# The second unit's columns move from the plain mixing stage to the seven-product stage

## Chip, cores and metric

The kernel runs on one core of a Trainium2 chip. The metric is the device time of one execution in microseconds (us); lower is better. A core has a matrix engine (PE, with its weight loads shown apart as PEld), three elementwise engines (DVE, ACT, POOL), and DMA queues that SP and ACT issue.

## What is computed

The input is `x` of 8 batches x 3008 tokens x 256 channels. The reference is a spectral block, then a token and channel mixer:

```
X = np.fft.rfft(x, axis=1)
Yr = Xr @ w_r - Xi @ w_i + b_r
Yi = Xr @ w_i + Xi @ w_r + b_i
...
x = np.fft.irfft(soft_threshold(Y), n=3008, axis=1)
h = np.maximum(x.transpose(0, 2, 1) @ w_tok1, 0.0) @ w_tok2
u = x + h.transpose(0, 2, 1)
out = u + np.maximum(u @ w_ch1, 0.0) @ w_ch2
```

`w_ch1` is 256 x 1536 and `w_ch2` 1536 x 256. Every product is made of three matmuls (`mm3`): high part by high part, high by low, low by high.

## The kernel before

The eight batches form five **units**: unit 0 is batch 0, unit 1 is batch 1, and units 2, 3 and 4 are two batches each. Each unit passes through two kinds of work.

The **spectral** work (generator `spectral(u)`) turns a unit's tokens into `b_d[u]` (the inverse transform's first half, in DRAM) and into `g_d[u]` (the rectified token product, in DRAM). For unit 1 it begins with thirteen steps of a transform of 47 points (`dft47`, line 299). Then come twelve steps for unit 1 and twenty-four for a later unit: `forward` (tile `px`, line 492), `mix` (tiles `pm`, lines 206 to 208), `inverse` (tile `pi`) and `tokens` (tile `gp`). Beside the steps of units 1 to 3 the next unit's 47-point transform is made (`beside`, tile `p`). Each step loads from DRAM and stores to it: `a_d`, `in_x`, `w_d` and `in_e` for unit 1, `ws_d` and `es_d` for the later units.

The **mixing** work takes a unit's columns (tokens) in chunks. Groups of 4 or 5 slots of 94 tokens (`groups`, cut by `sizes`) are made by `half_u`: token product and inverse transform in one PSUM bank (`pu`, or `sz` in the later stage), copied to `uf`. Then a chunk goes through `w_ch1` and `w_ch2`, in one of two ways:
- **plain** (`channel`): chunks of at most 512 columns. Per chunk, 12 blocks of `first` (tile `ph`) and `second` (tile `po`), with 72 + 72 matmuls as wide as the chunk. ACT makes `hh` and DVE `hlo` of each block.
- **seven-product** (`channel7`): chunks of at most 1024 columns, each cut in halves of columns, channels and hidden rows, with seven products of quarters for eight (a Strassen-Winograd scheme). Per chunk, 6 pairs x 2 layers x 7 products x 3 = 252 matmuls of half the chunk's width. The sums run on DVE, ACT and POOL. Its weight sums are made once, by `weigh` and `weigh2`, beside the last plain chunk (tiles `a`, `sf`, `ws`, lines 1028 to 1049); there the spectral pools are closed too (`open_seven`), and the new chunk's first operands are made (`first_u`, `rest_u`: tiles `t` and `ub`).

Engines run their instructions in the order in which they stand in the program, which a loop at the program's end sets. It walks through the chunks and, between pieces of a plain chunk, takes pieces of the spectral stream `sp` while the stream's remaining estimated cost (`left_s`) is over `pace` times the mixing's remaining cost (`left_c`). A piece that says "wait" or "rest" holds the stream back for 10 or 4 us of mixing. Whatever of the stream is left when the last plain chunk has begun is emitted in one go (`run(sp)`), since the seven-product stage runs with the spectral pools closed. Before the loop, `begin` makes unit 0's spectral work and the weights, and starts unit 1's transform.

Before the change the plain chunks are the seven of unit 0 (four of 470 columns, three of 376) and three of unit 1 (292, 512 and 512 columns). The other 1692 columns of unit 1 (844 + 848), and all of units 2 to 4, are seven-product chunks. The pacing has two laps: one over unit 0's chunks with `2.1 * SPECTRAL`, one over unit 1's plain chunks with the rest.

Of the kernel before, what the change touches and what calls it, by code (L numbers as in the profile page):

```python
# [23 lines left out]
UNITS = [[0], [1]] + [[2 * p, 2 * p + 1] for p in range(1, NP)]  # L24
# [8 lines left out]
CW = 512  # L33
# [4 lines left out]
CW7 = 2 * CW  # L38
SLOW = 1.75
SPECTRAL = 70.3 + NG * (SLOW - 0.7)  # L40
# [95 lines left out]
def tile_kernel(ctx: ExitStack, tc: tile.TileContext, io):  # L136
# [298 lines left out]
    gts = [None] * len(UNITS)  # L435
# [370 lines left out]


    outv = io["out"].rearrange("(t p) b n -> b p t n", p=128)
    sizes = {u: (4, 5, 5, 5, 4, 5, 4) if u == 1 else (5, 5, 5, 5, 4, 4, 4) for u in range(len(UNITS))}
    groups = [(u, b, sum(sizes[u][:i]), k) for u, bs in enumerate(UNITS) for b in range(len(bs)) for i, k in enumerate(sizes[u])]  # L810
    chunks = []
    for u, bs in enumerate(UNITS):
        total, at = N * len(bs), 0
        if u == 0:
            widths = [k * TOKS for k in sizes[u]]
        elif u == 1:
            widths = [292, 512, 512, 844, 848]
        else:
            plain = 0 if u == 2 else 0
            rest = total - plain  # L820
            widths = [plain % CW] * (plain > 0) + [CW] * (plain // CW) + [rest % CW7] + [CW7] * (rest // CW7)
        for cw in widths:
            chunks.append((u, at, cw))
            at += cw
        assert at == total
# [515 lines left out]
    def run(gen):  # L1341
        for _ in gen:
            pass


    sp = spectral(1)
    done = begin(sp)
    sp = chain(sp, *(spectral(v) for v in range(2, len(UNITS))))
    spent, left_s, left_c, pace, hold = done, 0.0, 0.0, 0.0, None
    first_wide = min(n for n, (_, _, cw) in enumerate(chunks) if cw > CW)  # L1350

    def mixing(lo, hi):
        slots = sum(groups[g][3] for n in range(lo, hi) for g in needs[n + 1])
        return sum(32.7 * cw / CW for _, _, cw in chunks[lo:hi]) + 3.6 * slots * TOKS / GW

    for n, (u, at, cw) in enumerate(chunks):
        if n == first_wide:
            channel7(range(n, len(chunks)))
            break
        if at == 0 and u < 2:  # L1360
            if u == 0:
                left_s = 2.1 * SPECTRAL - spent
                left_c = mixing(0, sum(cu == 0 for cu, _, _ in chunks))
            else:
                left_s = 3 * SPECTRAL + 4 * 70.3 - spent
                left_c = mixing(n, first_wide - 1)
            pace, hold = 0.0, left_c - (25.0 if u == 0 else 0.0)
        for c in channel(n):
            if c == "end":
                if chunks[n + 1][2] > CW:  # L1370
                    run(sp)
                    left_s = -1e9
                else:
                    while gts[u + 1] is None:
                        step = next(sp)
                        if step not in ("wait", "rest"):
                            left_s, spent = left_s - step, spent + step
                continue
            left_c -= c
            if hold is not None:  # L1380
                if left_c > hold:
                    continue
                pace, hold = left_s / max(left_c, 1.0), None
            while left_s > pace * left_c:
                step = next(sp, None)
                if step is None:
                    left_s = -1e9
                elif step in ("wait", "rest"):
                    hold = left_c - (10.0 if step == "wait" else 4.0)
                    break  # L1390
                else:
                    left_s, spent = left_s - step, spent + step
# [36 lines left out]
```

## Time and profile before

| | |
|---|---|
| median of 3 runs | 2319.94 us (2318.87 to 2321.26) |
| the profiled execution | 2317.41 us |
| its span, first to last instruction | 2315.6 us |
| granted PE clock | 0.999 |
| `begin`, to the first `ph` matmul | 0 to 152 us |
| plain chunks with the spectral stream | 152 to 948 us |
| rest of the last plain chunk, opening of the seven-product stage | 948 to 993 us |
| seven-product chunks | 993 us to the end |

The page gives the busy time of each engine, then the span in 40 slices, then the DMA queues, the chain of work that ended last, and the costliest groups of instructions. A matmul's duration on the page includes the pipeline's latency and overlaps the next one's. What a matmul costs a busy PE is the distance between the starts of two successive ones, read from the timeline.

### The profile page before, as it was taken

The numbers are of one execution on the slowest core, as the hardware profiler recorded it, in microseconds if no ns is written. First come the engines' busy times: TensorE is split into PE (matmuls) and PEld (weight loads), VectorE is DVE, ScalarE is ACT, GpSimd is POOL, SyncE is SP. The second block draws the span as 40 slices with busy tenths as digits, with TensorE's granted clock in tenths as the row PEclk, the third lists the DMA queues.
The fourth block names the chain that finished last, engine by engine and source line by source line (L and its number), as shares of the span: only waits on it lengthen the run. The fifth ranks groups of instructions, "written<-read, shape, count | busy, mean of one in ns | idle before, by whom it ended". The sixth has DMA issues, their size and how long they took to land.

```text
span 2315.6 us, 35046 instructions
## 1 busy us (share of the span) xinstructions
PE 2280.4 (98%) x12272; PEld 2000.0 (86%) x12272; DVE 1675.6 (72%) x2755; ACT 1442.7 (62%) x2660; POOL 1296.4 (56%) x1069
## 2 busy tenths in 40 slices
PE   8999999999999999999999999999999999999998
PEld 7778899999889989889988888898888889888876
DVE  7976766657667666767677777777777777777877
ACT  6764555445445544467677777667677766767776
POOL 0000333233334334157787888778788877878885
PEclk9999999999999999999999999999999999999999
DMA  8876566656656554422222202222221122222100
GB/s 220 252 240 188 151 220 207 217 180 204 205 188 224 186 194 158 137 73 66 78 65 69 64 22 81 69 84 62 70 64 41 62 69 85 62 69 64 59 1 37
DMA packets 150076, 277.22 MB, mean 120 GB/s; under 512 B 10965, under 2 KB 95533, under 8 KB 149901
## 3 DMA queue, kind: packets, MB, share of 16 engines
q1 hardware_dynamic: 115513, 208.40, 29.8%
q10 hardware_dynamic: 34388, 66.60, 8.5%
q8 instruction: 97, 1.59, 0.3%
q14 instruction: 78, 0.64, 0.1%
HBM read 177.57 MB, written 97.39 MB: 119 GB/s over the span
## 4 chain that ended last, share of the span: by engine, by line
PE 66%; DVE 4%; ACT 1%; issue 1%; POOL 0%; DVEq 0%; ACTq 0%; POOLq 0%
PE l L132 14%; PE sx L132 13%; PE sz L132 10%; PE sy L132 9%; PE sw L132 7%; PE px L492 2%; PE pm L208 1%; PE pm L206 1%; PE pm L207 1%; PE gp L207 1%; DVE ts L1132 1%; PE gp L208 1%; PE gp L206 1%; DVE ub L158 1%; PE pi L207 0%
## 5 line engine op out<-in xcount | busy, mean ns | idle before, releaser
L1129 POOL TENSOR_TENSOR op<-ts,op 128x512 fp32r<-128x512 f32 (+3 forms) x479 | 599.4, 1273 | 267.7 <-ACT op L1162 265.2
L1162 ACT ACTIVATE op<-ts 128x512 fp32r<-128x512 f32 (+3 forms) x480 | 293.4, 613 | 58.9 <-DVE ts L1132 45.6
L1129 DVE TENSOR_TENSOR uf<-sy,uf 128x512 f32<-128x512 f32 (+3 forms) x221 | 146.9, 665 | 213.0 <-PE sy L132 212.6
L132 PE MATMUL l<-op,ws 128*128 128x512 f32 (+3 forms) x1080 | 296.0, 382 | 0.0
L132 PEld LDWEIGHTS l<-op,ws 128*128 128x128 f32 x1080 | 202.8, 188 | 34.9
L1158 ACT ACTIVATE x<-sx 128x512 f32<-128x512 f32 (+3 forms) x240 | 139.9, 583 | 129.5 <-PE sx L132 128.7
L132 PE MATMUL sx<-ub,w 128*128 128x512 f32 (+3 forms) x720 | 198.8, 384 | 1.7 <-DVE ts L1132 1.0
L132 PE MATMUL sx<-ub,ws 128*128 128x512 f32 (+3 forms) x720 | 197.5, 383 | 1.6 <-ACT x L1158 1.6
L159 POOL TENSOR_TENSOR yl<-z,yh 128x512 fp32r<-128x512 f32 x72 | 93.9, 1304 | 183.0 <-ACT yh L156 176.4
L159 POOL TENSOR_TENSOR xtl<-xs,xth 128x256 fp32r<-128x256 f32 x84 | 69.6, 829 | 215.2 <-ACT xth L156 170.0
L132 PEld LDWEIGHTS sx<-ub,w 128*128 128x128 f32 x720 | 134.7, 188 | 27.7 <-DVE ts L1132 3.1
L132 PEld LDWEIGHTS sx<-ub,ws 128*128 128x128 f32 x720 | 135.1, 188 | 25.3 <-ACT x L1158 2.0
L1129 POOL TENSOR_TENSOR op<-b,op 128x512 fp32r<-128x512 f32 (+3 forms) x120 | 150.8, 1257 | 0.7 <-PE sy L132 0.4
L206 PE MATMUL pm<-wmh,xth 128*128 128x256 f32 x504 | 146.1, 290 | 1.9 <-ACT xth L156 1.3
L208 PE MATMUL pm<-wmh,xtl 128*128 128x256 f32 x504 | 142.8, 284 | 1.2 <-POOL xtl L159 1.2
L207 PE MATMUL pm<-wml,xth 128*128 128x256 f32 x504 | 142.3, 283 | 0.0
L1129 DVE TENSOR_TENSOR x<-sw,x 128x512 f32<-128x512 f32 (+3 forms) x120 | 80.7, 672 | 85.1 <-PE sw L132 85.1
L1182 ACT ACTIVATE x<-x 128x512 f32<-128x512 f32 (+3 forms) x120 | 74.1, 617 | 101.0 <-DVE x L1129 101.0
L132 PE MATMUL sy<-op,w2h 128*128 128x512 f32 (+3 forms) x442 | 134.1, 384 | 1.4 <-DVE uf L1129 1.4
L159 POOL TENSOR_TENSOR wt<-aw,wt 128x512 fp32r<-128x512 f32 x12 | 18.3, 1523 | 206.5 <-ACT wt L156 206.5
L941 DVE SCALAR_TENSOR_TENSOR hlo<-ph,hh 128x470 fp32r<-128x470 f32 (+3 forms) x120 | 72.1, 603 | 51.1 <-ACT hh L940 50.9
L940 ACT ACTIVATE hh<-ph 128x470 fp32r<-128x470 f32 (+3 forms) x120 | 63.5, 532 | 72.2 <-PE ph L208 61.9
(221 smaller groups left out, 6740.7 us busy)
## 6 DMA issues: line engine op xcount, KB each, us to landing
wt<-wt_d SPq DMA_DIRECT2D x28, 940.0 KB, 5.5
x<-in_x SPq DMA_DIRECT2D x39, 480.0 KB, 5.5
a<-a_d SPq DMA_DIRECT2D x36, 512.0 KB, 4.3
wt<-ws_d SPq DMA_DIRECT2D x36, 512.0 KB, 4.0
b_d<-bt ACTq DMA_DIRECT2D x36, 512.0 KB, 5.5
a_d<-a ACTq DMA_DIRECT2D x36, 480.0 KB, 3.8
wt<-wt_d SPq DMA_DIRECT2D x21, 752.0 KB, 5.0
b<-b_d SPq DMA_DIRECT2D x32, 480.0 KB, 6.2
```

The source lines that it names most:

```text
L132: return lambda *args, **kw: self.tc.keep_in_program_order(op(*args, **kw))
L159: lo_eng.tensor_tensor(out=lo, in0=src, in1=hi.bitcast(F32), op=ALU.subtract)
L206: PE.matmul(out, lhsT=wh, rhs=xh, start=start, stop=False, skip_group_check=more)
L207: PE.matmul(out, lhsT=wh, rhs=xl, start=False, stop=False, skip_group_check=more)
L208: PE.matmul(out, lhsT=wl, rhs=xh, start=False, stop=stop, skip_group_check=more)
L492: PE.matmul(pt[:, o:o + 128], lhsT=x, rhs=f2cols(2 * kp + ab), start=True, stop=True)
L940: S.activation(out=hh, in_=pt, func=AF.Relu)
L941: V.scalar_tensor_tensor(out=hlo, in0=pt, scalar=0.0, in1=hh.bitcast(F32), op0=ALU.max, op1=ALU.subtract)
L1129: eng.tensor_tensor(out=out, in0=in0, in1=in1, op=op)
L1158: pins[key] = S.activation(out=t, in_=src, func=func)
L1162: pins[k] = S.activation(out=ops[k][:, 0], in_=v[k] if src is None else src, func=AF.Copy if k[0] == "t" else AF.Relu)
L1182: pins["x2r"] = S.activation(out=v["x2"], in_=v["x2"], func=AF.Relu)
```

## The change

```diff
-    sizes = {u: (4, 5, 5, 5, 4, 5, 4) if u == 1 else (5, 5, 5, 5, 4, 4, 4) for u in range(len(UNITS))}
+    sizes = {u: (5, 5, 5, 5, 4, 4, 4) for u in range(len(UNITS))}
...
         if u == 0:
             widths = [k * TOKS for k in sizes[u]]
-        elif u == 1:
-            widths = [292, 512, 512, 844, 848]
         else:
-            plain = 0 if u == 2 else 0
-            rest = total - plain
-            widths = [plain % CW] * (plain > 0) + [CW] * (plain // CW) + [rest % CW7] + [CW7] * (rest // CW7)
+            widths = [total % CW7] + [CW7] * (total // CW7)
...
-        if at == 0 and u < 2:
-            if u == 0:
-                left_s = 2.1 * SPECTRAL - spent
-                left_c = mixing(0, sum(cu == 0 for cu, _, _ in chunks))
-            else:
-                left_s = 3 * SPECTRAL + 4 * 70.3 - spent
-                left_c = mixing(n, first_wide - 1)
-            pace, hold = 0.0, left_c - (25.0 if u == 0 else 0.0)
+        if n == 0:
+            left_s = 3 * SPECTRAL + 4 * 70.3 - spent
+            left_c = mixing(0, first_wide - 1)
+            pace, hold = 0.0, left_c - 25.0
         for c in channel(n):
             if c == "end":
-                if chunks[n + 1][2] > CW:
-                    run(sp)
-                    left_s = -1e9
-                else:
-                    while gts[u + 1] is None:
-                        step = next(sp)
-                        if step not in ("wait", "rest"):
-                            left_s, spent = left_s - step, spent + step
+                run(sp)
+                left_s = -1e9
                 continue
```

Unit 1's chunks become 960, 1024 and 1024 columns, all seven-product. Its groups keep their number (four of 5 slots, three of 4) in another order. The last plain chunk is now unit 0's last, of 376 columns, and the whole stream of units 1 to 4 is paced over the six chunks ahead of it. Lines after 815 of the program move up, by 4 (by 14 in the loop at the end).

Three places in the program show what moved.

**SP's queue in the twelve steps of unit 1's spectral work.** `a`, `x`, `aw` and `ef` are the loads of a step; `raw`, `wt_d`, `b` and `out` belong to unit 0's mixing. Before:

```order
L470 DMA a_3305<-a_d_91 128x2x256
L860 DMA wt_d<-wt_3076 512x1x376
L370 DMA ef<-in_e 128x256
L462 DMA x<-in_x 120x1024
L353 DMA aw<-w_d 128x512
L470 DMA a_3442<-a_d_91 128x2x256
L370 DMA ef<-in_e 128x256
L353 DMA aw<-w_d 128x512
L874 DMA b_3559<-b_d_92 96x4x256
L462 DMA x<-in_x 120x1024
L189 DMA raw<-in_wt 128x752
```

Now:

```order
L470 DMA a_2708<-a_d_91 128x2x256
L353 DMA aw<-w_d 128x512
L462 DMA x<-in_x 120x1024
L370 DMA ef<-in_e 128x256
L470 DMA a_2819<-a_d_91 128x2x256
L462 DMA x<-in_x 120x1024
L353 DMA aw<-w_d 128x512
L370 DMA ef<-in_e 128x256
L189 DMA raw<-in_wt 128x940 x2
L353 DMA aw<-w_d 128x512
```

The steps' own loads stand closer together; fewer loads of the mixing lie between them.

**DVE's queue in the opening of the seven-product stage**, where `a`, `sf` and `ws` are the weight sums, `hlo` a block of the last plain chunk, and `t` and `ub` the first operands of the new chunk, which need the groups of the new chunk. The first of them that need all its groups, before:

```order
L159 TENSOR_TENSOR ws<-sf,ws 128x6x128
L941 SCALAR_TENSOR_TENSOR hlo<-ph,hh 128x512
L1043 TENSOR_TENSOR a<-w2h,w2l 128x1024
L941 SCALAR_TENSOR_TENSOR hlo<-ph,hh 128x512
L1075 TENSOR_TENSOR t<-uf 128x422
L159 TENSOR_TENSOR ub<-t,ub 128x422
L1081 TENSOR_TENSOR t<-uf 128x422
```

Now:

```order
L1028 TENSOR_TENSOR sf<-a,sf 128x2x128
L1039 TENSOR_TENSOR a<-w2h,w2l 128x1024
L1071 TENSOR_TENSOR t<-uf 128x480
L159 TENSOR_TENSOR ws<-sf,ws 128x6x128
L159 TENSOR_TENSOR ub<-t,ub 128x480
L1077 TENSOR_TENSOR t<-uf 128x480
L937 SCALAR_TENSOR_TENSOR hlo<-ph,hh 128x376
```

Before, the new chunk needed two groups (`needs`), and `t` stood behind 23 rows of DVE work, counted from the first `a`; now it needs three groups, and `t` stands behind 37 rows.

**PE's queue where the spectral stream ends** (`gp` is its last product, `ph` the plain chunk). Now:

```order
L206 MATMUL gp<-yh,wt 128x512
L207 MATMUL gp<-yl,wt 128x512
L208 MATMUL gp<-yh,wt 128x512
L206 MATMUL ph<-uh,w_963 128x376
L207 MATMUL ph<-ul,w_963 128x376
L208 MATMUL ph<-uh,w_963 128x376
```

All of the last plain chunk, 144 matmuls of 376 columns and three groups, stands behind the stream's end. Before, its first block stood ahead of some 130 us of spectral work, and what stood behind were 138 matmuls of 512 columns and two groups.

## The prediction

> **What bounds the kernel now.** I read the page's busy shares and slices first, then the chain that ended last.
>
> ```profile
> PE 2280.4 (98%) x12272; PEld 2000.0 (86%) x12272; DVE 1675.6 (72%) x2755; ACT 1442.7 (62%) x2660; POOL 1296.4 (56%) x1069
> PE   8999999999999999999999999999999999999998
> DMA  8876566656656554422222202222221122222100
> PE 66%; DVE 4%; ACT 1%; issue 1%; POOL 0%; DVEq 0%; ACTq 0%; POOLq 0%
> ```
>
> PE is busy in every slice, and the chain lies on PE almost alone. Since an average hides stages, I then asked for the busy time in stretches: unit 1's spectral steps beside plain chunks (240 to 420), the start of unit 4's steps (820 to 840), unit 4's steps with no mixing beside them (840 to 930), and seven-product chunks (1000 to 1400).
>
> ```profile
> 240.00:420.00 180.00, 179.50 (x1119) 168.19 (x1118) 124.78 (x205) 92.34 (x177) 58.39 (x45) 1.00 0.67 207
> 820.00:840.00 20.00, 18.22 (x133) 16.52 (x133) 15.89 (x28) 9.54 (x21) 7.58 (x8) 1.00 0.36 133
> 840.00:930.00 90.00, 89.76 (x617) 83.14 (x616) 61.94 (x106) 42.42 (x89) 34.92 (x35) 1.00 0.49 167
> 1000.00:1400.00 400.00, 399.74 (x2020) 354.73 (x2020) 292.66 (x481) 280.98 (x522) 317.18 (x266) 1.00 0.23 68
> ```
>
> The columns after the length are busy us of PE, PEld, DVE, ACT and POOL, then the granted clock, the DMA share and GB/s. PE is full in both kinds of mixing and in spectral work alone. So a matmul removed is time removed, unless another engine or DMA comes up in its place, and spectral work does not need mixing beside it to keep PE full.
>
> **The matmuls.** First the counts of one line and form, then how far apart starts lie.
>
> ```profile
> L206 PE MATMUL po<-hh,w2h 128*128 128x512 f32 x48 | 19.1, 399 | 0.0
> L206 PE MATMUL po<-hh,w2h 128*128 128x292 f32 x24 | 7.1, 294 | 0.0
> L132 PE MATMUL l<-op,ws 128*128 128x422 f32 x54 | 13.3, 355 | 0.0
> 561.13 0.30 PE L206 MATMUL ph<-uh,w 128*128 128x292 f32 x1
> ...
> 562.74 1.05 PE L492 MATMUL px<-f,a 128*128 128x128 f32 x8
> 505.08 0.34 PE L206 MATMUL ph<-uh,w 128*128 128x376 f32 x1
> ...
> 505.95 0.34 PE L208 MATMUL ph<-uh,w 128*128 128x376 f32 x1
> 948.21 0.39 PE L206 MATMUL ph<-uh,w 128*128 128x512 f32 x1
> ...
> 956.37 0.37 PE L206 MATMUL pu<-wt,gh 128*128 128x470 f32 x1
> ...
> 961.09 0.48 PE L206 MATMUL ph<-uh,w 128*128 128x512 f32 x1
> 1017.35 0.74 PE L132 MATMUL sx<-ub,w 128*128 128x422 f32 x3
> 1017.93 0.74 PE L132 MATMUL l<-op,ws 128*128 128x422 f32 x3
> 1101.28 0.74 PE L132 MATMUL sx<-ub,w 128*128 128x424 f32 x3
> 1101.86 0.74 PE L132 MATMUL sw<-ub,ws 128*128 128x424 f32 x3
> 1125.24 0.77 PE L132 MATMUL sw<-ub,w 128*128 128x448 f32 x3
> 1125.85 0.77 PE L132 MATMUL sy<-ub,w 128*128 128x448 f32 x3
> 1301.51 0.84 PE L132 MATMUL sw<-ub,w 128*128 128x512 f32 x3
> 1302.19 0.84 PE L132 MATMUL sy<-ub,w 128*128 128x512 f32 x3
> ```
>
> A plain chunk has six such groups: 6 x 24 = 144 matmuls of 292 columns, 6 x 48 = 288 of 512. Twelve of 292 columns lie between 561.13 and 562.74: 0.134 us each. Of 376 columns, five starts later is 0.87 us later: 0.174. Thirty-six of 512 lie between 948.21 and 956.37: 0.227 us. In the seven-product stage, three matmuls of 422 or 424 columns take 0.58 us (0.193 each), three of 448 0.61 (0.203), three of 512 0.68 (0.227). For 480 I take the middle of 0.203 and 0.227: 0.215.
>
> - Removed: 144 x 0.134 = 19.3, 288 x 0.227 = 65.4, and the two odd wide chunks, 2 x 252 x 0.193 = 97.3. Together 182.0 us.
> - Added: a chunk of 960 columns, 252 x 0.215 = 54.2, and two of 1024, 504 x 0.227 = 114.4. Together 168.6 us.
> - Net **-13.4 us**. At 0.227 us per 512 columns, 18 of 144 matmuls less on 1316 columns would be 10.5 us; the other 3 us come from form, since a narrow matmul costs more per column.
>
> The groups (`pu`, later `sz`) keep their number and sizes, so they only move: nothing. The Trainium skill's page "TensorE: Matmul & The Clock Gate" (section "Wait — 56ns, not 53.3ns?") says that a warm matmul of N columns costs N / 2.4 GHz plus some 2.5 ns; by it, an estimate, the same sum would be 170.2 - 159.8 = 10.4 us saved, and the time 3 us later than I say. The trace has 227 ns where that gives 216, so I keep the rows.
>
> **The opening of the seven-product stage.** This is the one place where another engine already leads.
>
> ```profile
> 960.00:970.00 10.00, 8.16 (x38) 6.61 (x37) 9.86 (x18) 4.90 (x9) 0.00 (x0) 0.91 0.41 116
> 990.00:1000.00 10.00, 7.02 (x32) 5.42 (x31) 8.58 (x16) 6.73 (x14) 1.96 (x2) 1.00 0.14 52
> 955.59 1.23 DVE L1028 TENSOR_TENSOR a<-w 128x1024 f32<-128x1024 f32 x1 [1.77 <-DMA g_d<-gl]
> 993.36 0.42 DVE L159 TENSOR_TENSOR w2l<-sf,w2h 128x256 fp32r<-128x256 f32 x1
> 960.25 0.52 SPq L850 DMA_DIRECT2D wt<-wt_d  x1
> ```
>
> DVE works without a break from 955.6 (7.4 us after the stream's last product) to 993.8, and PE waits 1.84 + 2.98 us. PE's work behind the stream was 138 x 0.227 plus a group of 5 slots at 4.7 (956.37 to 961.09) and one of 4 at about 4, so 40 us; now it is 144 x 0.174 plus 3 x 4.7, so 39 us. DVE's work shrinks by about 1 us (narrower `hlo`). But `t` and the last `ub` now wait for the third group, and its load (`wt`, one buffer) can only be issued when the second group is done, as at 960.25. Ahead of that group's end stand 108 of the 144 matmuls and three groups, 33 us, and I add 3 us of waits for `hlo` and `wt`: 36 us after the stream's end. Behind `t` stand nineteen rows of DVE work ahead of the new stage's, some 11 us by their durations, so DVE ends at about 47 us and not at 45.6, with 1 to 2 us less PE work inside. Bounds: -1 us (DVE just does its shorter work) to +8 us (the queue stands still for two more loads of 4 us each). I take **+3 us**.
>
> **The dense spectral stream.** In the order of PE, the mixing that stands between the first and the last product of unit 1's twelve steps falls from some 103 us to some 30 us, beside 78 us of spectral matmuls that stay. So the stretch that took about 180 us (240 to 420) should take about 108. DVE's part of it, 125 us before, falls to about 84 (the rows of its queue between the same two places, at the trace's durations), so DVE does not lead. DMA is closer:
>
> ```profile
> raw<-in_wt SPq DMA_DIRECT2D x8, 470.0 KB, 4.5
> wt_d<-wt SPq DMA_DIRECT2D x4, 940.0 KB, 6.8
> b<-b_d SPq DMA_DIRECT2D x32, 480.0 KB, 6.2
> out<-o SPq DMA_DIRECT2D x4, 470.0 KB, 4.2
> 20.00:25.00 5.00, 4.08 (x35) 3.66 (x35) 3.54 (x9) 2.47 (x5) 0.00 (x0) 1.00 1.01 234
> 410.00:425.00 15.00, 15.00 (x104) 15.00 (x103) 8.86 (x15) 6.81 (x15) 2.71 (x2) 1.00 1.04 386
> ```
>
> 180 us at 207 GB/s are 37.3 MB. A chunk of mixing moves 2 x 470 + 940 + 480 + 470 KB, 2.8 MB, in some 35 us; 73 us less mixing are 5.9 MB less. So 31.4 MB in 108 us, 291 GB/s. The share, scaled by bytes, is 0.67 x 180 x 31.4 / 37.3 = 102 us of 108: near full. A full share moved 386 GB/s at 410 to 425 with PE unharmed, but 234 at 20 to 25 with PE waiting. The loss lies between 0 and 12 us; the sustained rows with PE full are the nearer ones, so I take **+2 us** for late loads.
>
> **Where a wait goes.** Unit 4's start lost 1.8 us of PE (820 to 840): its first steps ran in the last lap, with no mixing beside them. Now the stream ends ahead of the last chunk, and the "wait" and "rest" holds put 14 us of unit 0's mixing beside that start. Gain between 0 and 3 us; I take **-1.5 us**.
>
> **Sum.** -13.4 + 3 + 2 - 1.5 = -9.9 us. Against the profiled execution of 2317.41 (span 2315.6 and 1.8 around it) that is 2307.5. The runs' median, 2319.94, lies 2.5 above it, and a new median will likely do so too: **2310 us**.
>
> **Rivals.**
> 1. *DMA takes over in unit 1's steps* (ends slower). If the transfers run at the 234 GB/s of the row at 20 us, 31.4 MB take 134 us in place of 108: +26, less the +2 already in, so 2334. It decides at 31.4 MB / (108 + 12) us, about 262 GB/s: below that nothing is left of the gain. For it: small packets there (unit 1 alone has rows of one batch), and loads only one step ahead, so PE stands behind each late one. Against: 386 GB/s in a full share, and only 0.5 us of PE lost in 180 us so far. Chance 0.08.
> 2. *The opening eats most of it.* Three groups with one `wt` buffer beside a full DVE: +8, with dense steps +5 in place of +2: 2318, no change that can be told. For it: PE already waits there. Against: DVE's work is no longer than before. Chance 0.13.
> 3. *The change does not do what it says*: the seven-product stage follows POOL (317 us busy of 400), so that more of its columns cost more than 0.227 us a matmul, and the time is 2320. Against: PE had 399.74 of those 400 us. It is inside the 0.13.
> 4. *Nothing is lost*: -13.4 - 3 - 1 gives 2303. It lies inside the forecast's case.
>
> **How the numbers follow.** A measurement of this kernel can tell about 0.2% (4.6 us) from no change. The forecast's case, 2303 to 2315, has chance 0.79 and is faster; rival 2 with 3 has 0.13, within 0.2%; rival 1 has 0.08, slower. The range leaves the ends out: 2304 to 2319.
>
> **What would show it.** After: seven-product chunks begin near 903 us where they began at 993 (84.7 us of plain matmuls and some 9 us of groups less ahead of them, 3.5 us of losses more), and take about 1403 us in place of 1323 (168.6 - 97.3 of matmuls and two groups more). PE stays above 97% in slices up to the opening; a DMA share near 1 with PE below 9 there is rival 1; PE waiting over 8 us between the stream's last `gp` and the first `sx`, ended by `ub` or `t`, is rival 2; spacing over 0.23 us in the seven-product stage is rival 3. An opening of about 44 us shows my +3 too high. The forecast is wrong if PE's removed time does not come back within 5 us.

## The result and the profile after

| | before | after |
|---|---|---|
| median of 4 runs each, in turn | 2319.40 us (2318.81 to 2321.26) | 2345.50 us (2342.19 to 2347.96) |
| ratio, 95% interval | 1 | 1.0110 (1.0093 to 1.0128) |
| profiled execution, span | 2317.41, 2315.6 | 2345.68, 2343.9 |
| granted PE clock, mean | 0.999 | 0.994 |
| first product of the seven-product stage | 990.6 | 933.4 |

The change makes the kernel 26 us slower. The prediction was 2310 us, faster, with a range to 2319: it was wrong, in sign too. First the page's busy shares, its slices of PE and DMA and the chain that ended last, after the change.

```profile
PE 2284.2 (97%) x12092; PEld 1979.5 (84%) x12092; DVE 1718.1 (73%) x2788; ACT 1478.5 (63%) x2700; POOL 1371.7 (59%) x1112
PE   8999988999999999999999999999999999999998
DMA  8876775766666444122212112222210222222100
PE 66%; DVE 6%; ACT 1%; issue 1%; POOL 0%; DMA 0%; DVEq 0%; ACTq 0%; POOLq 0%
```

PE's row has eights in the sixth and seventh slices (293 to 410 us), where all was 9. A digit is coarse, and a slice is 59 us wide; the stretches that the prediction asked for say more (length, busy us of PE, PEld, DVE, ACT, POOL, granted clock, DMA share, GB/s).

```profile
140.00:240.00 100.00, 94.79 (x503) 82.49 (x503) 72.01 (x132) 53.06 (x98) 12.71 (x9) 0.97 0.66 199
240.00:420.00 180.00, 162.98 (x1000) 145.90 (x999) 122.06 (x182) 89.16 (x174) 71.43 (x55) 0.96 0.72 224
420.00:880.00 460.00, 453.49 (x2893) 416.37 (x2894) 318.22 (x516) 229.46 (x452) 167.66 (x152) 1.00 0.61 195
1000.00:1400.00 400.00, 399.87 (x1931) 340.11 (x1930) 296.04 (x467) 282.84 (x506) 322.76 (x258) 1.00 0.22 65
```

From 240 to 420 PE idles 17 us where it idled 0.5, and its clock is 0.96. The seven-product stage is as full as before. Busy time hides a slow clock, so for the comparisons below I use one measure, called **PE loss**: for each two successive matmuls, the distance of their starts less the median distance of that form in the same trace, summed over a stretch. It counts gaps and slow matmuls alike (opening: 880 to 1000 us). Each loss below comes from the one profiled execution of its kernel; the executions of one kernel differ by some us (the changed kernel's from 2342 to 2348), so differences of 2 or 3 us between two losses say little.

| PE loss, us | 0-150 | 150-250 | 250-400 | 400-880 | opening | behind it | all |
|---|---|---|---|---|---|---|---|
| before | 10.8 | 2.7 | 1.1 | 7.8 | 9.2 | 12.6 | 44.3 |
| after | 10.7 | 10.0 | 28.3 | 11.6 | 8.3 | 16.6 | 85.5 |

41.2 us more are lost, 34.5 of them from 150 to 400 us: unit 1's first stage, its twelve steps (their last product is at 355.8), and the start of unit 2. The span grew by 28.3 only; 28.3 - 41.2 = -12.9 us is what the matmuls saved.

### The profile page after: what moved, and what is told of

Same layout as the page of the kernel before. It is cut to its first block, busy times and chain, and to the rows that moved or that the text cites. A ratio compares the mean times of both kernels' runs of the same rounds, so it can differ in the third digit from the quotient of the medians.

```text
span 2343.9 us, 34879 instructions
## 1 busy us (share of the span) xinstructions
PE 2284.2 (97%) x12092; PEld 1979.5 (84%) x12092; DVE 1718.1 (73%) x2788; ACT 1478.5 (63%) x2700; POOL 1371.7 (59%) x1112
## 4 chain that ended last, share of the span: by engine, by line
PE 66%; DVE 6%; ACT 1%; issue 1%; POOL 0%; DMA 0%; DVEq 0%; ACTq 0%; POOLq 0%
PE l L132 14%; PE sx L132 13%; PE sz L132 10%; PE sy L132 10%; PE sw L132 7%; PE px L492 1%; DVE ts L1128 1%; DVE ub L158 1%; PE pm L208 1%; PE pm L207 1%; PE pm L206 1%; PE gp L207 1%; PE gp L208 1%; PE gp L206 1%; DVE uf L1125 0%
## 5 line engine op out<-in xcount | busy, mean ns | idle before, releaser
L1125 POOL TENSOR_TENSOR op<-ts,op 128x512 fp32r<-128x512 f32 (+2 forms) x503 | 639.1, 1295 | 280.3 <-ACT op L1158 276.6
L1158 ACT ACTIVATE op<-ts 128x512 fp32r<-128x512 f32 (+2 forms) x504 | 311.3, 619 | 65.5 <-DVE ts L1128 50.5
L1125 DVE TENSOR_TENSOR uf<-sy,uf 128x512 f32<-128x512 f32 (+2 forms) x232 | 156.0, 672 | 222.4 <-PE sy L132 221.9
L132 PE MATMUL l<-op,ws 128*128 128x512 f32 (+2 forms) x1134 | 314.3, 385 | 0.0
L1154 ACT ACTIVATE x<-sx 128x512 f32<-128x512 f32 (+2 forms) x252 | 148.7, 590 | 138.7 <-PE sx L132 138.2
L132 PE MATMUL sx<-ub,w 128*128 128x512 f32 (+2 forms) x756 | 211.4, 388 | 3.2 <-DVE ts L1128 2.4
L132 PE MATMUL sx<-ub,ws 128*128 128x512 f32 (+2 forms) x756 | 210.5, 387 | 2.9 <-ACT x L1154 2.9
L1125 POOL TENSOR_TENSOR op<-b,op 128x512 fp32r<-128x512 f32 (+2 forms) x126 | 161.0, 1278 | 0.5 <-PE sy L132 0.2
L132 PE MATMUL sy<-op,w2h 128*128 128x512 f32 (+2 forms) x464 | 142.0, 387 | 1.4 <-DVE uf L1125 1.4
L132 PE MATMUL l<-op,w2h 128*128 128x512 f32 (+2 forms) x334 | 110.0, 410 | 0.0
```

Of the source, the lines that this page charges most:

```text
L132: return lambda *args, **kw: self.tc.keep_in_program_order(op(*args, **kw))
L1125: eng.tensor_tensor(out=out, in0=in0, in1=in1, op=op)
L1154: pins[key] = S.activation(out=t, in_=src, func=func)
L1158: pins[k] = S.activation(out=ops[k][:, 0], in_=v[k] if src is None else src, func=AF.Copy if k[0] == "t" else AF.Relu)
```

## Where PE stands, read once in full

The granted clock dips at four places of this stretch. Three of them, in windows of 5 us:

```profile
195.00:200.00 5.00, 2.89 (x15) 2.14 (x13) 3.03 (x6) 2.73 (x5) 0.00 (x0) 0.83 0.90 267
200.00:205.00 5.00, 3.80 (x12) 3.04 (x13) 3.62 (x8) 2.21 (x4) 1.61 (x1) 0.50 0.73 229
325.00:330.00 5.00, 3.18 (x21) 2.67 (x19) 4.85 (x11) 0.73 (x2) 1.25 (x1) 1.00 0.92 323
330.00:335.00 5.00, 4.35 (x20) 3.69 (x21) 4.75 (x6) 2.57 (x7) 4.35 (x4) 0.64 0.32 107
355.00:360.00 5.00, 4.88 (x27) 4.09 (x26) 0.00 (x0) 0.59 (x1) 0.00 (x0) 1.00 1.03 370
360.00:365.00 5.00, 2.53 (x7) 2.17 (x8) 2.51 (x5) 2.54 (x6) 0.00 (x0) 0.71 0.96 335
```

At these three the DMA share is at 0.9 or above, ACT is busy 0.6 to 2.7 of 5 us, PE loses time, and then the granted clock falls. (The fourth place, at 389, has a share of 0.62 and is the start of unit 2.) A high share alone does not do it: from 260 to 265 and from 280 to 285 it was 1.01 and 1.00, and PE was busy for all of 5 us. At the first place PE waits 1.45 us for ACT's `xh`, which stands behind a copy that waits 2.61 us for a store. At the second it waits 1.82 us for DVE's `xs`, and no transfer is named: DVE worked without a break from 318 to 330 us, nine of its rows on `wide`, which is made of the mixing's `raw`. At the third place the timeline of ACT tells what stands between DMA and PE (start, duration, what, and in brackets the idle time before it with what ended it):

```profile
348.50 0.59 ACT L559 COPY bt<-pi 128x512 f32<-128x512 f32 x1 [0.84 <-DMA a_d<-a]
348.74 0.33 ACTq L386 DMA_DIRECT2D ws_d<-wt  x1
349.12 2.10 ACTq L560 DMA_DIRECT2D b_d<-bt  x1
...
354.47 0.62 ACTq L560 DMA_DIRECT2D b_d<-bt  x1
359.33 0.59 ACT L559 COPY bt<-pi 128x512 f32<-128x512 f32 x1 [5.93 <-DMA b_d<-bt]
...
361.58 0.38 ACT L583 ACTIVATE gh<-gp 128x256 fp32r<-128x256 f32 x1 [1.66 <-DMA es_d<-et]
361.86 1.01 ACT L936 ACTIVATE hh<-ph 128x470 fp32r<-128x470 f32 x2
```

The copy to `bt` needs a buffer whose store has not landed, and ACT stands 5.93 us. Everything behind it on ACT is late: the next store, `gh`, which by the profile waits 1.66 us more for another store, and `hh`, which has nothing to do with either. PE, at the same time:

```profile
359.30 0.37 PE L207 MATMUL ph<-ul,w 128*128 128x470 f32 x1
359.51 0.38 PE L208 MATMUL ph<-uh,w 128*128 128x470 f32 x1
362.47 0.76 PE L206 MATMUL po<-hh,w2h 128*128 128x470 f32 x1 [2.59 <-ACT hh L936]
363.03 0.60 PE L206 MATMUL ph<-uh,w 128*128 128x470 f32 x1
363.42 0.59 PE L207 MATMUL ph<-ul,w 128*128 128x470 f32 x1
363.81 0.59 PE L208 MATMUL ph<-uh,w 128*128 128x470 f32 x1
```

It waits 2.59 us for `hh`, and then the same matmul that stood 0.21 us apart (359.30 to 359.51) stands 0.39 apart. So here late stores cost an engine that works in order, then PE, then PE's clock. Over 150 to 400, in windows of 5 us, length times (1 - granted clock) sums to 10.2 us, and to 0 before.

## Experiments

Three theories for the lost time. **T1**: DMA is too full when unit 1's steps are dense, so transfers land late. **T2**: ACT's queue, which holds both stores and work that PE needs, with two buffers for what is stored. **T3**: the chain of engines in a step (what each one hands to the next) is too long for a dense order, transfers or not. Ahead of these: is it the pace of the stream or the columns? All ratios are to the kernel before, run in turn on the same chip, with 95% intervals; losses are PE loss in us at 150-250, 250-400 and 400-880.

| label | median us | ratio | losses |
|---|---|---|---|
| e2 | 2351.66 | 1.0139 (1.0119 to 1.0159) | 11.6, 26.3, 12.4 |
| e1d | 2344.13 | 1.0107 (1.0086 to 1.0128) | 3.4, 2.4, 35.9 |
| e1c | 2321.43 | 1.0010 (0.9998 to 1.0023) | 3.3, 3.6, 16.8 |
| e5b | 2334.55 | 1.0070 (1.0052 to 1.0088) | 11.2, 15.0, 13.7 |
| e5a | 2335.61 | 1.0066 (1.0036 to 1.0095) | 12.6, 13.0, 12.3 |
| e7 | 2336.60 | 1.0074 (1.0050 to 1.0098) | 4.0, 25.5, 11.7 |
| e12 | 2325.30 | 1.0025 (1.0010 to 1.0041) | 4.9, 15.0, 14.5 |
| e6 | 2342.59 | 1.0088 (1.0064 to 1.0111) | 12.8, 20.0, 14.6 |
| e10 | 2344.91 | 1.0097 (1.0060 to 1.0134) | 11.0, 27.6, 12.2 |
| g3 | 2345.52 | 1.0119 (1.0097 to 1.0141) | 11.5, 23.8, 16.3 |
| e11 | 2331.50 | 1.0053 (1.0033 to 1.0073) | 3.7, 3.8, 19.2 |
| g1 | 2329.16 | 1.0057 (1.0040 to 1.0074) | 2.0, 12.1, 16.7 |
| f1 | 2333.46 | 1.0056 (1.0040 to 1.0071) | 8.9, 7.1, 19.4 |
| f2 | 2339.43 | 1.0087 (1.0069 to 1.0106) | 4.3, 14.8, 21.5 |
| g2 | 2320.58 | 1.0014 (1.0002 to 1.0026) | 4.0, 3.9, 14.6 |
| g4 | 2327.13 | 1.0043 (1.0028 to 1.0058) | 3.0, 2.8, 22.1 |
| h1 | 2325.63 | 1.0030 (1.0021 to 1.0039) | 5.5, 2.4, 20.2 |
| h2 | 2329.06 | 1.0043 (1.0028 to 1.0059) | 4.7, 2.8, 22.6 |

### Pace or columns: e2, e1d, e1c

e2 is the kernel before with the changed pace:

```diff
-        if at == 0 and u < 2:
-            ...
+        if n == 0:
+            left_s = 3 * SPECTRAL + 4 * 70.3 - spent
+            left_c = mixing(0, 6)
+            pace, hold = 0.0, left_c - 25.0
```

> The kernel before (its columns, five plain chunks more narrow) with the changed kernel's pace: the whole spectral stream beside unit 0's mixing. If the pace is the whole loss and the columns a gain of about 13 us: 2350 to 2362 us. If the columns are what costs, 2318 to 2325 us.

2351.66 us: the pace is the whole loss (37.9 us lost at 150 to 400, where the changed kernel lost 38.3). Its profiled span is 2353.2, 37.6 above before's, and the changed kernel's 2343.9 is 9.3 below that; the medians differ by 6.2. So the columns seem to gain some 6 to 9 us beside the same pace; by the times alone that is not clear of noise, since the intervals of the two ratios overlap (1.0119 to 1.0159 and 1.0093 to 1.0128).

e1d and e1c keep the changed columns and give unit 1 a thinner pace (e1c: over chunks 0 to 3; e1d: `5` and `1.7` in place of `4` and `1.6`):

```diff
-            left_s = 3 * SPECTRAL + 4 * 70.3 - spent
-            left_c = mixing(0, first_wide - 1)
+            left_s = 1.6 * SPECTRAL - spent
+            left_c = mixing(0, 4)
             pace, hold = 0.0, left_c - 25.0
+        elif n == 4:
+            left_s = 3 * SPECTRAL + 4 * 70.3 - spent
+            left_c = mixing(4, first_wide - 1)
+            pace, hold = left_s / left_c, None
```

> The changed kernel's columns, but two paces for the spectral stream in place of one: unit 1's steps spread over chunks 0 to 4 (about as thin as before the change), units 2 to 4 packed beside chunk 5 and its sequel. If the density of unit 1's steps is what costs 40 us (T1 bandwidth, T2 ACT's queue with its stores, T3 chain of latencies, all three alike here), nearly all of it goes: 2306 to 2316 us, PE excess between 150 and 420 us below 10. If any dense spectral step costs, the loss only moves to units 2 to 4: 2335 us or more, with the lost time behind 450 us.

> The same with unit 1's steps over chunks 0 to 3 and units 2 to 4 over chunks 4 and 5. If the loss grows smoothly with the density of unit 1's steps, between e1d and the change: 2312 to 2325 us. If there is a threshold (a bandwidth that is just exceeded), about as e1d or better: 2306 to 2316.

In both, the loss of 150 to 400 us goes (38.3 to 5.8 and 6.9). But in e1d the time comes back, as its second case had it: 24 us more are lost at 400 to 880, most of them at the starts of units 2 to 4, and 9.7 in the middle of unit 2's steps (440 to 530), where only 24 of 523 matmuls are mixing. In e1c a smaller part does. Both of e1c's cases took e1d for the better of the two; it was the other way. The density of unit 1's steps costs; and so do the starts of the later units when little mixing is left for them.

### Bytes, issues or buffers: e5b, e5a, e7, e10, e6, e12, g3

All of these are edits of the changed kernel with its dense pace. e5b drops the stores of all pairs of split weights and exponentials but the first, e5a keeps their issues and cuts their bytes. In both, the later units load the first pair each time, so the loads keep their bytes:

```diff
 e5b
+            if kp == 0:
                 PUT.dma_start(out=kept[kp], in_=...)
 e5a
+            part = slice(0, flat.shape[1] if kp == 0 else 64)
+            PUT.dma_start(out=kept[kp][:, part], in_=flat[:, part])
 both
-            DMA.dma_start(out=..., in_=kept[kp])
+            DMA.dma_start(out=..., in_=kept[0])
```

> The changed kernel without unit 1's stores of the split weights and exponentials (11 of 12 pairs left out, 8.4 MB of the 31.4 MB of unit 1's steps; the loads of units 2 to 4 stay, all from the first pair, so its output is another). T1 (DMA bandwidth): 23 MB in 108 us need 213 GB/s, below what any row showed as harmful, so the loss of unit 1's steps (some 25 of 40 us) goes: 2312 to 2325 us. T2 (ACT issues 22 stores fewer, of 0.3 to 2 us each): as much or a little less, 2318 to 2332 us. T3 (latency of the chain of engines, no transfer in it): no change, 2340 to 2348 us.

> As e5b (loads of units 2 to 4 all from the first pair), but the 22 stores of later pairs are still issued, each of 64 elements a partition in place of 1024 and 512: their bytes go, ACT's issues and their order stay. The profile's PE loss of 150 to 400 us (excess over each matmul form's median spacing: 38.3 us in the changed kernel, 26.2 in e5b) decides. If the bytes were what e5b saved (T1): about as e5b, 24 to 29 us, 2331 to 2338 us. If ACT's issues were (T2): 34 to 40 us, 2340 to 2348 us.

e5a saves as much as e5b (13.0 and 15.0 us left of 28.3 at 250 to 400). ACT's issues of stores took 24 us of that stretch in e5a and 12 in e5b, after 30 in the changed kernel, so between these two the bytes count and the issues don't. That is T1 against T2's issue time. The whole loss of 150 to 400 fell to 25.6 and 26.2. e5b's time, 2334.55, lies in none of the ranges given for it: more came back than T3 had, less than T1 or T2.

e7 leaves out the stores of unit 1's first stage (its second stage loads as many bytes from another array, so nothing waits for these stores either); e10 keeps them and doubles the distance at which a copy meets its buffer's last store:

```diff
 e7
+        if pool is None and w == C:
+            return
         PUT.dma_start(out=rows[...], in_=a[:n * KH])
 e10
+        if pool is None and w == C:
+            if g % 2 == 0:
+                wc["a"] = ev([120, 2, 2, w], "a")
+            a = wc["a"][:, g % 2]
```

> The changed kernel without the stores of unit 1's first stage (13 of 240 KB), its second stage loads the same number of bytes from another array, so the output is another. If ACT's copies that wait for a store to land are what costs in unit 1's first stage: the loss of 150 to 250 us falls from 10.0 to 2 to 4 us, 2336 to 2341 us. If the chain of engines is (sum and difference, split by ACT and DVE, three products, copy), it stays at 8 to 12 us and the time at 2341 to 2348 us.

> The changed kernel with unit 1's first-stage copies written to two halves of each store buffer, so that a copy waits for the store four groups earlier in place of two; no byte and no issue changes. If the wait for the landing costs: as e7, loss of 150 to 250 us at 2 to 5 us, 2336 to 2342 us. If it only hides the chain's own latency: 8 to 12 us, no change in the time.

Without the stores the first stage loses 4.0 in place of 10.0 us. With the longer distance it loses 11.0, although the wait that I had in mind is gone. ACT's waits from 170 to 250 us in the changed kernel (total us, times, longest), then the same in e10:

```profile
ACT hh L936 <- PE ph L208: 11.6, 11, 2.1
ACT a L281 <- DMA a_d<-a: 8.9, 7, 2.6
```

```profile
ACT hh L941 <- PE ph L208: 9.8, 10, 2.1
ACT a L286 <- PE p L208: 7.8, 7, 1.8
ACT uf L904 <- PE pu L898: 6.6, 4, 1.8
ACT wide L170 <- DMA raw<-in_wt: 2.4, 1, 2.4
```

No copy waits for a store any more; in its place ACT stands 2.4 us behind a group's load. So in the first stage the wait that the trace named was not the cause, and T2 as a matter of buffers alone ends there. The wait for a buffer of `bt`, read above at 359, was not lifted by any run. And e7 does not tell bytes from the rest: it takes away the stores' bytes, their issues, and also SP's waits for their landing (10.7 us in the changed kernel from 170 to 250).

e6 issues the split weights' stores from SP; e12 has both cuts of bytes; g3 moves POOL's last link of the forward product to DVE (`G` becomes `V` in one `split`):

```diff
 e6
-            PUT.dma_start(out=kept[kp], in_=...)
+            DMA.dma_start(out=kept[kp], in_=...)
```

> The changed kernel with the stores of the split weights and exponentials issued by SP's queue in place of ACT's; all bytes stay, ACT loses 24 issues of 0.3 to 2 us. T2 (ACT's queue): the loss of 150 to 400 us falls to about e5b's 26 us, 2331 to 2338 us. T1 (bytes): it stays at 36 to 40 us, 2341 to 2348 us; more than that if SP, which issues every load in order, now stands behind stores that wait for their data.

> The changed kernel with both cuts of e5a and e7: unit 1's first-stage stores left out (its second stage loads from another array), and of the split weights' stores only 64 elements a partition stay. If the two savings simply add: a loss of 16 us (12 to 20) of the 38.3 at 150 to 400 us, 2320 to 2327 us. If bandwidth is all and there is a threshold: below 8 us, 2312 to 2319 us. If a chain of engines is the floor: above 20 us, 2328 us or more.

> The changed kernel with the last third of each forward product's split (its low part) on DVE in place of POOL; POOL is what PE waited for longest in the dense steps by the profile (4.3 us), DVE is busy 97 of 150 us there. If the chain of engines (T3) is the rest of the loss: 28 us at 250 to 400 fall to 22 or less, 2336 to 2341 us. If DMA sets the steps' length and POOL is only the last in line: 26 to 31 us, 2341 to 2349 us.

e6 lost 8 us less at 250 to 400 and 5.8 more in the two stretches beside it; its time can't be told from the changed kernel's. Its 32.8 us at 150 to 400 lie between its two cases (26, and 36 to 40), so that ACT's issues cost nothing is not shown. e12's 19.9 us at 150 to 400 is near the sum of both savings, at the edge of the range given: the stores make 18.4 of the 34.5 us, 12.7 of them by bytes alone (e5a). Of the 15.0 left at 250 to 400, 5.8 lie at 370 to 380 and 390 to 400, the start of unit 2 beside little mixing. g3 saved 4.5 us there and nothing in time, between its two cases; so T3 is open in size.

How long transfers took to land agrees with T1. From 240 to 420 before, the median from issue to landing was 3.2 us for a store of `bt` and 5.7 for a load of `x`; from 245 to 365 in the changed kernel it was 6.9 and 7.0, in e5a 5.8 and 6.3, and in the thin e1c (245 to 395) 3.5 and 5.6. What PE waited for longest in the changed kernel at 150 to 420 was several engines' work in turn:

```profile
PE pm L208 <- POOL xtl L159: 4.3, 7, 1.6
PE po L206 <- ACT hh L936: 3.8, 2, 2.6
PE p L206 <- ACT xh L156: 2.3, 4, 1.4
PE pm L206 <- ACT xth L156: 2.2, 1, 2.2
```

### Traffic alone: e11, g1

Cutting bytes also shortens queues. The reverse test adds bytes that nobody reads to e1c, whose steps are thin:

```diff
 e11
+                if u == 1:
+                    for i in range(2):
+                        DMA.dma_start(out=more_d[n, i], in_=io["x"][i, n])
 g1
+                if kp > 1:
+                    for i in range(2):
+                        DMA.dma_start(out=more_d[kp, i], in_=ws_d[kp - 2])
```

> e1c (unit 1's steps spread over four chunks, a loss of 3.6 us at 250 to 400) with two copies of 480 KB from DRAM to DRAM added in each of unit 1's twelve steps, issued by SP, whose data nobody waits for: 11.5 MB more in some 155 us, which makes about 306 GB/s asked for, as much as in the changed kernel's dense steps. T1 (DMA is what limits): the loss of 250 to 400 us comes back, 12 us or more, and the time rises from 2321 to 2330 us or more. T2 and T3 (ACT's queue, the chain of engines): at most 3 us more, 2319 to 2326 us.

> e1c with two DRAM to DRAM copies of 512 KB of the split weights stored a step earlier, in each of unit 1's steps from the third on; they can't run ahead of these stores, so at least 16 of 20 (8.4 MB) lie in the stretch of 240 to 395 us, which then asks for some 285 GB/s, as the dense steps did. Nobody waits for the data. T1 (DMA limits by itself): the loss of 250 to 400 us rises from 3.6 to 12 us or more, 2330 us or more. T2 and T3: 6 us at most, 2319 to 2327 us.

e11 did not test its stretch, and its 2331.50 us, in T1's range, is no proof of T1 there: its copies have no input to wait for, and SP issued them from 34 to 116 us, during `begin`. There they did harm: loss at 0 to 150 rose from 11.5 to 18.4 us, with e1c first and e11 second here.

```profile
60.00:120.00 60.00, 56.28 (x301) 47.09 (x301) 55.56 (x114) 42.60 (x76) 0.00 (x0) 1.00 0.81 245
```

```profile
60.00:120.00 60.00, 53.73 (x275) 44.91 (x275) 53.52 (x106) 39.46 (x72) 0.00 (x0) 0.97 0.98 344
```

g1's copies depend on a store of the step before, and most ran in the steps (12 of 20 were issued from 280 to 360). e1c first, g1 second:

```profile
280.00:320.00 40.00, 40.00 (x256) 37.10 (x255) 26.26 (x38) 21.74 (x42) 16.43 (x14) 1.00 0.82 256
320.00:360.00 40.00, 39.54 (x242) 35.77 (x241) 30.84 (x49) 22.31 (x44) 15.26 (x12) 1.00 0.82 254
```

```profile
280.00:320.00 40.00, 40.00 (x256) 37.12 (x255) 26.71 (x41) 20.50 (x39) 16.66 (x14) 1.00 0.96 320
320.00:360.00 40.00, 35.67 (x209) 31.97 (x208) 25.80 (x42) 21.28 (x41) 13.83 (x10) 0.91 0.93 300
```

The loss of 250 to 400 rose from 3.6 to 12.1 us, as T1 said; the time, 2329.16, is just below the 2330 that I gave for it. But traffic is not all that was added. The copies stand in SP's queue, which issues in order and waited 31.6 us from 240 to 400 for the stores that they read, ahead of the steps' loads; whether that delayed loads which PE then missed was not tested. e11's copies, which wait for nothing, are the cleaner test, in another stretch. Note the first pair: a share of 0.96 for 40 us cost PE nothing, and 0.93 in the next 40 cost 4 us and a dip of the clock. A mean share does not tell which.

### Can both gains be had: f1, f2, g2, g4, h1, h2

e1c has the gain of the columns and a loss of 12.4 us at 400 to 600, where before had 0.8. f1 starts unit 2 at the thinner pace (`1.9` for `1.6`), f2 holds more mixing at units' starts (12 and 7 for 10 and 4), g2 is e1c with e6's edit, g4 is e1c with g3's, h1 and h2 are g2 with the held mixing in smaller pieces (in h2 more of it):

```diff
 h1 (h2: "lead" 10.0)
+    holds = {"wait": 10.0, "rest": 4.0, "lead": 6.0, "fill": 3.0}
 ...
+                if n < 3 and u >= 2:
+                    yield "fill"
```

> e1c with the first pace reaching 1.9 in place of 1.6 spectral units by the end of chunk 3, so that unit 2's first steps still have mixing beside them. e1c lost 12.4 us at 400 to 600 where before lost 0.8, most of it where unit 2 starts in dense order. If that start is the cause: a loss of 3 to 6 us there, 2311 to 2317 us. If the loss moves with the pace into unit 1's steps (some 19% denser): 8 us more at 150 to 400, 2319 to 2326 us.

> e1c with more mixing held beside each unit's start (12 and 7 in place of 10 and 4 units). If the starts of units 2, 3 and 4 lose for want of cover: the loss of 400 to 600 us falls from 12.4 to some 6, 2312 to 2318 us. If they lose since loads are late whatever lies beside: 2319 to 2325 us.

> e1c with the stores of the split weights and exponentials issued by SP in place of ACT (as e6 did with the dense pace, where the loss of 250 to 400 us fell from 28 to 20). If the start of unit 2 in e1c (7 us lost at 400 to 450) stands behind ACT's stores: 2312 to 2318 us, faster than before. If not: 2319 to 2325 us.

> e1c with the same move from POOL to DVE. If units 2 to 4, packed beside less mixing, lose by POOL's link of the chain: 2313 to 2318 us. If DVE becomes the later one or nothing changes: 2319 to 2326 us.

> g2 with the mixing that is held beside the start of units 2 to 4 put in four pieces (6 units ahead of the first step, 3 after each of the first three) in place of two (10 and 4). If the filling of each unit's pipeline costs the 10 us of 400 to 600: 4 to 6 us there, 2310 to 2316 us, faster than before. If the packing costs as such: 9 to 13 us, 2317 to 2324 us.

> The same with 10 units ahead of the first step, 19 a unit in place of 15, so that units' later steps have almost no mixing beside them (in e1c such steps lost nothing: under 0.1 us at 450 to 550 and 600 to 700). If filling is the cause: as h1 or 1 to 2 us better, 2309 to 2315 us. If later steps need the mixing: the loss moves to 600 to 880 us, 2318 us or more.

None beats before; e1c and g2 end within 0.2% of it by their medians. f1, f2, g4 and h1 ended above both of their cases, by 1 to 14 us; g2 and h2 fell into their slower ones. f1 and f2 made unit 1 denser again (f2's holds apply to it too), and the loss came back there: 16.0 and 19.1 at 150 to 400. h1 did what it was meant for at 400 to 600 (7.3 after g2's 10.3), and paid at unit 4's start, for which less mixing was left (12 of 174 matmuls from 735 to 770, where g2 has 47 of 231). g2 first, h1 second:

```profile
740.00:760.00 20.00, 17.87 (x134) 16.84 (x133) 14.57 (x25) 8.49 (x19) 5.99 (x7) 1.00 0.59 215
```

```profile
740.00:760.00 20.00, 15.55 (x96) 14.00 (x95) 10.02 (x18) 6.55 (x15) 3.42 (x4) 0.83 0.73 258
```

By these runs mixing beside the stream is cover: unit 1's steps lose less with it (e1c, e1d), and so do the later units' starts (h1). That it covers late transfers in the one and the filling of a unit's pipeline in the other is argued, not shown. The change takes some 94 us of it away (84.7 us of plain matmuls and two groups), and wherever the rest was put here, some place went without. That no order exists which beats before was not shown; six tries did not find one.

## Why the prediction was wrong, step by step

- **The matmuls** (-13.4): right. The span and the losses give -12.9. The seven-product stage took 1410 us, near the 1403 given, but began at 933 in place of 903.
- **The opening** (+3): too high. From the stream's last product to the first of the new stage it took 40.6 us, after 42.6. PE loss there fell by 0.9. DVE ended its weight sums 45 us behind the stream, where 47 was expected. Its longest wait is now behind ACT, as the waits of 886 to 960 show:

```profile
PE sx L132 <- ACT x L1154: 2.9, 1, 2.9
PE po L207 <- DVE hlo L937: 0.8, 1, 0.8
```

- **Where a wait goes** (-1.5): not had. Unit 4's start still lost some 2 us, and units 2 and 3 now lose at theirs: 400 to 880 us cost 3.8 us more.
- **The dense spectral stream** (+2): this step failed, in its size and in the reason for it: it cost 34.5 us, where the bounds were 0 and 12. It had worked out 291 GB/s and 102 of 108 us of DMA time, "near full", and then took the bursts "with PE full" (386 GB/s for 15 us) as the nearer rows, which makes a full share harmless. Measured, with unit 1's steps in it:

```profile
245.00:365.00 120.00, 106.24 (x653) 94.28 (x652) 81.01 (x118) 61.48 (x120) 53.38 (x40) 0.96 0.83 259
```

259 GB/s, below the 262 at which rival 1 was said to decide; a low rate says only that the same bytes took longer, and the share was 0.83, not 1. From the first product of `mix` to the last of `tokens` (228.5 to 355.8) unit 1's steps took 127 us at 240 GB/s: 108 us of work, as forecast, and 20 of loss. So rival 1 had the place and, as far as e5a shows it, the mechanism, at a chance of 0.08; its price of 26 us was near for the steps and too low for the change. Missing were unit 1's first stage (7.3 us more, 6.0 of which go with its stores in e7), the end of the steps and the start of unit 2 (9 us from 355.8 to 400). PE's clock, which the prediction left out, is inside these losses.
- The inference behind it, "spectral work does not need mixing beside it to keep PE full", was read from the middle of unit 4's steps (840 to 930). It holds there; it did not hold at a unit's start, nor in e1d in the middle of unit 2's steps, and unit 1's steps lost 20 us beside some 34 us of mixing.
- Behind the opening 4.0 us more were lost than before; the runs don't say why; with the same columns e1c lost 15.5 there and g1 12.8, before 12.6.

Settled: the pace is the cause (e2, e1c). Unit 1's stores carry about half of what it costs (18.4 of 34.5 us in e12), at least 12.7 us of it by their bytes (e5a); that traffic by itself can cost PE time is shown in `begin` (e11) and, less cleanly, in the steps (g1). Open: the remaining 16 us at 150 to 400 in e12 over before, some 6 of them unit 2's start, and how the rest divides between ACT's queue, SP's queue, stretches of DVE without a break (as at 318 to 330) and the chain.

## What to carry to other kernels

Work that is moved beside less other work loses cover: price the stretch where it becomes dense by what its transfers need over that stretch, and take a DMA share near 1 as a possible cost, not as room, where loads and stores run only a step ahead of their use. When the trace names a wait for a store, ask which transfer is late next: in unit 1's first stage, lifting the one wait (e10) only showed the next. And a few microseconds of PE idling should be charged with the slow matmuls that follow.

## What the runs showed of the hardware

PE's clock fell to 0.50 of full speed after single gaps of PE: 2.59 us long at 359.5 (the clock fell while it lasted), 2.17 at 389.4, 1.82 at 327.9 and 1.45 at 195.8, and in the kernel before 1.84 at 965.3, where the mean of 960 to 970 is 0.91. It stayed there for 3.4 or 6.8 us, and matmuls of 470 columns then stood 0.39 us apart in place of 0.21. The Trainium skill ("TensorE: Matmul & The Clock Gate", "What's actually happening") has the clock at half rate after an idle window of about 3.4 us; the half rate agrees with 0.39 against 0.21, but none of these gaps was as long as that. Not every gap did it: in the kernel before, one of 1.63 us at 991.6 left 1.00 for 990 to 1000.

A store's issue on ACT in the changed kernel took 0.33 to 0.62 us as a rule and up to 2.47 from 250 to 400 (at 286.88; another took 2.10 at 349.12); in the kernel before none took longer than 0.62 in that stretch.
